# q and k of blocks 9 to 11 turned by transposing transfers on SyncE's queue

## The chip, the cores and the metric

One core of a Trainium2 chip. The metric is the device time of one execution in microseconds. TensorE (PE) multiplies and, in this kernel, also transposes; VectorE (DVE) and ScalarE (ACT) work on its results; GpSimd (POOL) and SyncE (SP) mostly issue transfers, each into a queue of its own that is worked off in order.

## The reference

Two stages. The first is a retention layer with a decaying state per head; the second a channel mix on its result. Batch 4, 8 heads, 768 tokens, head size 64; model width 512, hidden width 1024.

```python
for t in range(S):
    state = gamma[None, :, None, None] * state + np.einsum('bhd,bhe->bhde', k[:, :, t], v[:, :, t])
    y[:, :, t] = scale * np.einsum('bhd,bhde->bhe', q[:, :, t], state)
...
xk = mu_k * x + (1.0 - mu_k) * x_prev
xr = mu_r * x + (1.0 - mu_r) * x_prev
k = np.maximum(xk @ w_k, 0.0)
v = k * k @ w_v
r = 1.0 / (1.0 + np.exp(-(xr @ w_r)))
return (r * v)
```

## The kernel before, in words

The 4 x 768 tokens are cut into 12 blocks of 256 (three blocks to a batch, so 9, 10 and 11 are the last batch). The recurrence is done blockwise: inside a block as masked scores (k times q, masked, times v), from block to block through a carried state of 64x64 per head. Decay factors are put on v (`vs`), on the state (`G`, with the constants `gd`) and on the result (`gy`).

For a block, in short: `lq`, `lk`, `lv` load (the first two cast to fp16 on the way); `Tq`, `Tk` turn q and k on TensorE so that the head dimension lies on the partitions; `Eq`, `Ek` copy them from PSUM to the tiles `qT` and `kT` on ScalarE (L240); `S` are the scores (L317 for blocks 6 to 11), `M` the mask (L346); `C` is the block's own state (L365); `U` adds it to the carried one (L418), `G` decays that; `I` multiplies the carried state by q (L440), `Y` adds the scores times v (L461) and the other half of `I`; `D` scales into `xT`. Then the channel mix: `dx`, `X` (L557) mix tokens; `K` (L571, L581), `Qa` (L590), `Qb` (L598, L602) are the first product, the relu and the square; `R` (L611) and `s` (L617) the gate; `V` (L623) the second product, `O` (L629) the result, `st` (L636) the store.

Blocks 6 to 11 (`HALF`) do the first stage in 64x64 pieces, four of which use the four quarters of TensorE's array. Heads go in four pairs `j`; the partition half `a` of a head in a pair is given by `HEADS`. In odd pairs the two heads are swapped, so that in `I` the input half and the output half differ:

```python
HEADS = ((0, 1), (3, 2), (4, 5), (7, 6))
```

The whole program is one list, `ORDER`, written out by hand. A word is an operation, its block and further arguments; `~v`, `~a`, `~p`, `~s` name the engine (VectorE, ScalarE, GpSimd, SyncE), `@67` the PSUM banks. Words of one engine run in the order of the list, and each waits for its inputs and for the buffers that it overwrites. `qT` and `kT` have three buffers each, so block 10 takes the place of block 7, block 9 that of 6, block 11 that of 8. The results `os` have four. SyncE's queue carries the stores and, in the middle, `lv.11`; GpSimd's carries nearly all loads.

Of the kernel before, what the change touches and what calls it, by code (L numbers as in the profile page):

```python
# [10 lines left out]
F32 = mybir.dt.float32  # L11
# [11 lines left out]
HEADS = ((0, 1), (3, 2), (4, 5), (7, 6))  # L23
ORDER = """
cm gy.0~v mu~a lv.0~p lq.0.0.2~s lk.0.0.2~s ck.0.0.2~a cq.0.0.2~a z.12@6 Tq.0.0.2@0 Tk.0.0.2@1 gy.1~v
z.1@2 mt@2 Ek.0.0.2~a Eq.0.0.2~a S.0.1.0.2@01 S.0.0.0.2@45 me~a lk.0.2.4~p Tk.0.2.4@2 Ek.0.2.4~a
lq.0.2.4~p vs.0~v C.0@67 U.0.0~v Tq.0.2.4@3 Eq.0.2.4~a lq.1~p lk.1~p M.0.1.0.2~v z.2@2 S.0.1.2.4@23
U.0.1~v lv.1~p lk.2~p I.0@01 S.0.0.2.4@67 M.0.0.2.4~v wk.0~p wk.1~p G.0~a z.2@6 Tq.1@6 Eq.1~a vs.1~p
lq.2~p Tk.1@7 Ek.1~a M.0.0.0.2~v M.0.1.2.4~v Y.0 D.0~v t.0.0.3~a t.0.0.2~a t.0.0.1~a lv.2~p z.2@4
S.1.1@23 M.1.1~v C.1@01 U.1.0~v z.2@4 I.1@23 S.1.0@67 X.0.0.1~v t.0.1.2~a X.0.0.2~v Tk.2@0 t.0.1.3~a  # L30
t.0.0.0~a M.1.0~v X.0.0.0~v z.2@4 Y.1 t.0.1.1~a X.0.0.3~v Ek.2~a K.0.0@0 K.0.1@6 lq.4~p U.1.1~v
G.1~a wr~p lk.4~p D.1~v dx.1~v X.1.0.2~v X.1.0.0~v K.0.2@1 Qa.0.0~a Qb.0.0~a Qa.0.2~a lq.3~p
X.1.0.1~v X.1.0.3~v X.1.1.0~v Qa.0.1~a K.0.3@0 Qa.0.3~a lk.3~p vs.2~v Tq.2@1 X.1.1.2~v K.1.3@6
K.1.0@0 C.2@7 U.2.0~v lv.3~p Eq.2~a S.2.1@23 M.2.1~v S.2.0@45 M.2.0~v Qb.0.3~a lv.4~p K.1.1@1
X.1.1.1~v Qa.1.0~a t.0.1.0~a K.1.2@7 I.2@23 Qb.0.1~a Qa.1.1~a wv.0~p Qb.0.2~a Tq.4@01 Eq.4~a Y.2
Qa.1.3~a Qb.1.1~a X.0.1.3~v X.1.1.3~v R.1.1@4 Tk.4@01 Ek.4~a J.2 R.1.0@6 Qa.1.2~a s.1.0~a X.0.1.2~v
X.0.1.1~v X.0.1.0~v R.0.1@5 s.0.1~a s.1.1~a R.0.0@7 s.0.0~a S.4.1@01 Qb.1.0~a D.2~v dx.2~v X.2.0.2~v
X.2.0.0~v S.4.0@23 Tq.3@4 Eq.3~a X.2.0.1~v wv.1~p X.2.0.3~v Tk.3@7 lq.5~p Ek.3~a K.2.2@5 Qa.2.2~a
K.2.3@4 M.4.1~v M.4.0~v Qa.2.3~a Qb.2.3~a lk.6~p S.3.1@67 M.3.1~v S.3.0@01 vs.3~p C.3@23 U.3.0~a
Qb.2.2~a K.2.1@4 Qa.2.1~a K.2.0@2 Qa.2.0~a I.3@45 lq.6~p vs.4~v C.4@67 U.3.1~v X.2.1.1~v V.0.1.0@3  # L40
M.3.0~v V.1.0.0@2 G.3~a U.4.0~v I.4@01 X.2.1.3~v U.4.1~v J.3 Qb.1.3~a Y.4 Qb.2.0~a lk.5~p X.2.1.2~v
X.2.1.0~v Y.3 D.3~v dx.3~v V.0.0.0@7 V.0.1.1 O.0.1~v Tq.5@45 J.4 D.4~v dx.4~v R.2.0@6 Qb.2.1~a
V.0.0.1 O.0.0~v X.3.0.1~v Eq.5~a Qb.1.2~a V.1.0.1 X.3.0.2~v O.1.0~v Tq.6@01 Eq.6~a Tk.6@45 Ek.6~a
st.0.0~s lk.7~p st.1.0~s V.1.1.0@3 V.1.1.1 O.1.1~v s.2.0~a R.2.1@0 s.2.1~a lv.5~p X.3.0.0~v
X.3.0.3~v Tk.7@67 Ek.7~a G.4~a S.6@45 M.6~v Tk.5@23 Ek.5~a vs.5~v V.2.0.0@0 K.3.2@1 Qa.3.2~a K.3.0@6
S.5.0@23 M.5.0~v S.5.1@45 C.5@1 U.5.0~v K.3.3@7 Qb.3.2~a Qa.3.0~a lq.7~p K.3.7@6 Qa.3.3~a Qa.3.7~a
lv.6~p lq.8~p vs.6~v M.5.1~v V.2.0.1 st.0.1~s I.5@67 O.2.0~v st.2.0~s C.6@23 U.6.0~a U.6.1~v U.6.2~v
K.3.6@1 Qa.3.6~a lk.9~p X.3.1.3~v Y.5 Tq.7@45 Eq.7~a U.6.3~v X.3.1.2~v I.6@01 J.5 X.3.1.0~v D.5~v
X.3.1.1~v Qb.3.3~a G.6~a V.2.1.0@2 K.3.1@3 V.2.1.1 O.2.1~v Qb.3.7~a Qa.3.1~a Qb.3.1~a dx.5~v K.3.4@4
K.3.5@5 Qa.3.5~a X.5.0.0~v X.5.0.3~v R.3.1@2 s.3.1~a lv.7~p Qa.3.4~a X.5.0.1~v Qb.3.4~a R.3.0@5  # L50
R.4.0@2 s.3.0~a s.4.0~a Qb.3.0~a X.5.0.2~v vs.7~v K.5.2@4 S.7@67 st.1.1~s M.7~v Qb.3.5~a Y.6
Qb.3.6~a lv.10~p C.7@23 U.7.0~v X.5.1.1~v Qa.5.2~a K.5.0@5 R.4.1@6 Qa.5.0~a D.6~v s.4.1~a V.4.0.0@4
V.4.0.1 V.3.1.0@5 U.7.1~v Qb.5.0~a X.5.1.3~v U.7.2~v I.7@01 X.5.1.2~v U.7.3~v Tq.8@67 Eq.8~a
X.5.1.0~v O.4.0~v lv.8~p vs.8~v Qb.5.2~a lq.10~p lk.8~p Tk.8@23 Ek.8~a V.3.1.1 V.3.0.0@4 C.8@67
O.3.1~v st.2.1~s st.3.1~s Y.7 dx.6~v D.7~v Tq.10@23 V.3.0.1 Eq.10~a G.7~a dx.7~v X.6.0.2~v V.4.1.0@5
V.4.1.1 X.6.0.0~v R.5.0@0 R.5.1@1 K.5.3@2 Qa.5.3~a Qb.5.3~a O.3.0~v s.5.0~a K.5.1@4 X.6.0.1~v lq.9~p
lk.10~p Qa.5.1~a Qb.5.1~a lv.11~s s.5.1~a X.6.0.3~v K.6.3@2 Qa.6.3~a K.6.2@3 K.6.5@4 Qa.6.2~a
U.8.0~v Qa.6.5~a X.6.1.2~v V.5.0.0@0 st.3.0~s X.6.1.0~v K.6.4@1 Qa.6.4~a O.4.1~v U.8.1~v X.6.1.1~v
U.8.2~v I.8@45 S.8@67 Tk.10@23 Ek.10~a V.5.0.1 lv.9~p X.6.1.3~v vs.9~v K.6.6@1 Qb.6.2~a M.8~v
Qa.6.6~a Qb.6.5~a S.10@67 O.5.0~v Y.8 M.10~v D.8~v vs.10~v dx.8~v st.5.0~s st.4.0~s Tk.9@23 Ek.9~a  # L60
V.5.1.0@1 V.5.1.1 X.8.1.3~v vs.11~v O.5.1~v lk.11~p Qb.6.3~a Tk.11@23 Qb.6.4~a X.8.0.1~v X.8.0.3~v
lq.11~p Tq.11@67 Ek.11~a X.8.1.2~v Tq.9@45 Eq.9~a K.6.1@0 Qa.6.1~a Eq.11~a R.6.0@2 s.6.0~a K.6.7@4
R.6.1@5 s.6.1~a Qa.6.7~a C.9@23 S.11@67 X.8.0.0~v C.10@01 K.6.0@5 U.9.0~a Qa.6.0~a Qb.6.0~a U.9.1~v
X.8.0.2~v Qb.6.6~a U.9.2~v U.9.3~v G.9~v Qb.6.1~a R.7.0@4 s.7.0~a K.8.1@5 Qa.8.1~a K.8.0@3 Qa.8.0~a
R.7.1@2 s.7.1~a K.8.2@4 Qa.8.2~a V.6.0.0@3 U.10.0~v X.8.1.1~v U.10.1~v U.10.2~v st.4.1~s U.10.3~v
M.11~v G.10~v I.9@45 Qb.6.7~a C.11@67 S.9@01 M.9~v Qb.8.0~a V.6.0.1 V.7.1.0@2 V.7.1.1 U.11.0~v
U.11.1~v I.10@01 U.11.2~v I.11@67 O.6.0~v Y.9 D.9~v dx.9~v V.6.1.0@3 V.6.1.1 O.6.1~v K.8.3@4
Qa.8.3~a Qb.8.2~a Y.10 D.10~v dx.10~v X.9.0.3~v X.9.0.1~v X.9.0.0~v Y.11 X.9.0.2~v D.11~v st.5.1~s
st.6.1~s V.7.0.0@3 Qb.8.1~a V.8.0.0@4 V.8.1.0@5 Qb.8.3~a V.8.0.1 V.7.0.1 O.7.0~v O.7.1~v X.8.1.0~v
dx.11~v X.11.0.2~v V.8.1.1 K.9.4@0 K.9.6@1 K.9.5@6 Qa.9.5~a Qb.9.5~a K.9.1@3 K.9.7@2 Qa.9.7~a  # L70
Qb.9.7~a X.11.0.3~v X.11.1.0~v X.11.0.0~v R.8.0@6 K.9.0@2 s.8.0~a Qa.9.6~a Qa.9.0~a Qb.9.0~a K.9.2@7
K.9.3@1 Qa.9.2~a X.11.1.3~v X.11.0.1~v X.9.1.0~v K.11.0@2 Qa.11.0~a Qb.11.0~a R.8.1@7 Qb.9.2~a
s.8.1~a st.7.0~s st.6.0~s Qb.9.6~a O.8.0~v X.9.1.1~v K.11.3@2 K.11.1@4 X.9.1.2~v Qa.11.3~a X.9.1.3~v
R.10.1@7 K.11.2@6 R.9.1@2 Qa.9.3~a Qa.11.1~a O.8.1~v R.9.0@1 Qa.9.1~a Qb.9.1~a Qb.9.3~a V.9.1.0@3
Qb.11.1~a X.11.1.1~v X.11.1.2~v Qa.11.2~a V.10.0.0@4 V.10.1.0@6 Qa.9.4~a Qb.9.4~a V.10.1.1 R.11.0@0
s.9.0~a V.9.1.1 st.7.1~s V.9.0.0@1 V.9.0.1 st.8.1~s Qb.11.2~a V.10.0.1 s.9.1~a V.11.0.0@2 s.10.1~a
O.10.1~v O.9.1~v st.9.1~s R.10.0@3 O.9.0~v Qb.11.3~a st.9.0~s R.11.1@1 s.11.0~a V.11.0.1 st.10.1~s
Vc.11.1.1@0 O.11.0~v s.10.0~a st.8.0~s O.10.0~v s.11.1~a Oc.11.1.1~v Vc.11.1.0@1 st.10.0~s st.11.0~s
Oc.11.1.0~v sc.11.1.0~s sc.11.1.1~a
# [4 lines left out]
def kernel(  # L84
# [35 lines left out]
    gd_np = gam[np.array(HEADS).T[par // D]] ** TM  # L120
# [34 lines left out]
    csm = const.tile([P, 4 * H + (2 + LOG) * NJ + 2 * NCO + 3], F32, name="csm_sb")  # L155
# [15 lines left out]
    gd = csm[:, o : o + NJ]  # L171
    g0 = csm[:, o + NJ : o + 2 * NJ]
    pw = csm[:, o + 2 * NJ : o + (2 + LOG) * NJ].rearrange("p (l j) -> p l j", l=LOG)
    ident8 = csm[0 : 2 * NCO, o + (2 + LOG) * NJ : o + (2 + LOG) * NJ + 2 * NCO]
    mark = csm[:, o + (2 + LOG) * NJ + 2 * NCO :]
# [20 lines left out]
    def heads(j):  # L196
        return [(a, h, h // 2, h % 2) for a, h in enumerate(HEADS[j])]

# [21 lines left out]

    def load(x, d, split, a=None):
        def go(e, n, j0=0, j1=NJ):
            b, t0 = n // NB, n % NB * TM
            hs = slice(2 * j0, 2 * j1)
            src = x[b, hs, t0 : t0 + TM, :]
            dst = staged(a)[:, hs] if (a, n, j0) in EARLY else d(n)[:, hs]
            if split and (half(n) or wide(n)):
                for i in range(2):
                    e.dma_start(  # L229
                        out=dst[:, :, i * D : i * D + D],  # L230
                        in_=src[:, i * P : i * P + P].rearrange("h p d -> p h d"),
                    )
            else:
                e.dma_start(out=dst, in_=src.rearrange("h (p i) d -> p h (i d)", i=2))

        return go
# [26 lines left out]
    def trans(a):  # L263
        def go(e, n, j0=0, j1=NJ):
            pt = turned(n, a, j0)
            src = (K16 if a else Q16)(n)
            for j in range(j0, j1):
                for i in range(2):
                    if whole(n):
                        for s, h, jo, hp in heads(j):  # L270
                            nc.tensor.transpose(  # L271
                                pt[low(s), j, i, :], src[:, h, i * D : i * D + D], ident
                            )
                        continue
                    for u in range(2):
                        for s, h, jo, hp in heads(j):
# [19 lines left out]
    def turned_k(e, n, j0=0, j1=NJ):  # L296
# [6 lines left out]
        )  # L303

# [53 lines left out]
    def state_half(n):  # L358
        ps = banks("C", n).rearrange("p u (i j d) -> p u i j d", i=2, j=NJ)
        for j in range(NJ):  # L360
            for i in range(2):
                for u in range(2):
                    if more(n) or not (u and i):
                        for a, h, jo, hp in heads(j):
                            nc.tensor.matmul(  # L365
                                ps[low(a), u, i, j, :],
                                lhsT=K16(n)[low(u), h, i * D : i * D + D],
# [430 lines left out]
```

## Time and profile before

| | |
|---|---|
| runs | 153.82, 154.86, 154.31 us; median 154.31 |
| profiled execution | 154.38 us, of which the span is 152.6 us |
| TensorE busy | 144.1 us, 94% |
| VectorE busy | 128.7 us, 84% |
| ScalarE busy | 100.6 us, 66% |
| GpSimd busy | 55.3 us, 36% |
| chain that ended last | TensorE 91%, VectorE 3%, ScalarE 2% |
| DMA busy | 9 tenths or more up to about 84 us, little after |

The span is the time in the profiler's window; the execution's time has some 1.8 us around it. In the timelines, "PE" rows are matmuls, "PEld" weight loads, "SPq" rows the issuing of transfers by SyncE. A group's row gives its busy time, the mean length of one in ns, and after the bar the idle time ahead of it with what ended it.

### The profile page before, as it was taken

The page shows a single profiled execution, that of the slowest core. Times are in us where ns is not written, and L with a number is a line of the kernel's source. Part 1 is how long each engine was busy: PE and PEld are TensorE (multiplying, and loading weights), DVE is VectorE, ACT ScalarE, POOL GpSimd, SP SyncE. Part 2 cuts the span into 40 slices and gives each one's busy share as a digit, 9 for nine tenths or more (in the row PEclk, how much of TensorE's full clock was granted, in tenths as well). Part 3 has the DMA queues.
Part 4 walks back from the last instruction along what each step waited for, and adds up shares of the span by engine and source line. Part 5 has one row for each costly group of instructions (what it writes and reads, how often), then busy time and mean ns, then how long its engine had stood idle before and what let it go on. Part 6 is the DMA issues. An engine that isn't in the chain of part 4 may idle for free.

```text
span 152.6 us, 5532 instructions
## 1 busy us (share of the span) xinstructions
PE 144.1 (94%) x2426; PEld 82.9 (54%) x2426; DVE 128.7 (84%) x214; ACT 100.6 (66%) x187; POOL 55.3 (36%) x65
## 2 busy tenths in 40 slices
PE   7977799999999999999999999899999999999990
PEld 3354487758655554547554655557555445744450
DVE  7876999999999999999999999999789999702240
ACT  3466979899934894979483889879405048997130
POOL 7954988579867109997600000000000000000000
PEclk9999999999999999999999999999999999999999
DMA  5999999999999999999999203220002050010435
GB/s 137 215 224 200 207 229 194 170 249 210 196 167 207 236 250 112 290 275 203 206 191 225 83 0 136 81 73 0 4 4 75 0 205 1 14 54 4 158 117 206
DMA packets 45624, 22.16 MB, mean 145 GB/s; under 512 B 37400, under 2 KB 41248, under 8 KB 45600
## 3 DMA queue, kind: packets, MB, share of 16 engines
q0 software_dynamic: 38704, 14.42, 74.0%
q1 hardware_dynamic: 6592, 7.21, 13.7%
q8 instruction: 19, 0.31, 0.8%
q10 hardware_dynamic: 304, 0.18, 0.5%
q14 instruction: 5, 0.04, 0.1%
HBM read 24.16 MB, written 6.29 MB: 200 GB/s over the span
## 4 chain that ended last, share of the span: by engine, by line
PE 91%; DVE 3%; ACT 2%; issue 1%; DVEq 0%
PE ps L623 27%; PE ps L581 14%; PE ps L611 14%; PE ps L571 14%; PE ps L701 4%; PE ps L277 3%; PE ps L440 2%; PE ps L271 2%; DVE a L353 2%; PE ps L330 1%; PE ps L477 1%; ACT qT L240 1%; PE ps L317 1%; PE ps L461 1%; PE ps L641 1%; PE ps L365 1%
## 5 line engine op out<-in xcount | busy, mean ns | idle before, releaser
L623 PE MATMUL ps<-wv,k2s 128*128 128x512 f16 x184 | 43.3, 380 | 0.0
L590 ACT ACTIVATE kr<-ps 128x512 f32<-128x512 f32 x48 | 27.4, 596 | 21.5 <-PE ps L581 11.1
L623 PEld LDWEIGHTS <-k2s 128*128 128x128 f16 x184 | 17.0, 98 | 19.3 <-ACT k2s L602 0.2
L629 DVE SCALAR_TENSOR_TENSOR os<-ps,rs 128x512 f32<-128x512 f32 x23 | 15.5, 685 | 12.4 <-ACT rs L617 7.1
L611 PE MATMUL ps<-wr,xr 128*128 128x512 f16 x96 | 23.5, 379 | 0.0
L581 PE MATMUL ps<-xk,wk 128*128 128x256 f16 x192 | 23.4, 273 | 0.0
L571 PE MATMUL ps<-xk,wk 128*128 128x512 f16 x96 | 22.9, 379 | 0.0
L229 POOL DMA_DIRECT2D k<-in_k_dram x20 | 17.9, 908 | 11.1 <-PE ps L383 6.8
L581 PEld LDWEIGHTS <-wk 128*128 128x128 f16 x192 | 18.3, 98 | 4.4 <-issue 0.2
L240 ACT COPY qT<-ps 128x1024 f16<-128x1024 f16 (+1 forms) x13 | 12.4, 951 | 9.2 <-PE ps L277 7.8
L557 DVE SCALAR_TENSOR_TENSOR xr<-dx,mu,xT 128x256 f16<-128x256 f32 (+1 forms) x32 | 18.0, 579 | 0.1
L617 ACT ACTIVATE rs<-ps 128x512 f32<-128x512 f32 x24 | 13.7, 594 | 6.1 <-DVE os L629 3.2
L229 POOL DMA_DIRECT2D v<-in_v_dram x18 | 16.0, 904 | 3.6 <-DMA wr<-in_moe_w_r_dram 1.9
L557 DVE SCALAR_TENSOR_TENSOR xk<-dx,mu,xT 128x256 f16<-128x256 f32 (+1 forms) x32 | 17.1, 581 | 0.2
L353 DVE TENSOR_TENSOR a<-ps,c_sb 128x1024 f16<-128x1024 f32 (+1 forms) x14 | 14.6, 1066 | 0.7 <-PE ps L338 0.4
L602 ACT ACTIVATE k2s<-kr 128x512 f16<-128x512 f32 x24 | 14.6, 626 | 0.2
L571 PEld LDWEIGHTS <-wk 128*128 128x128 f16 x96 | 9.1, 98 | 10.3
L611 PEld LDWEIGHTS <-xr 128*128 128x128 f16 x96 | 9.1, 98 | 10.2 <-DVE xr L557 0.3
L598 ACT ACTIVATE k2s<-kr 128x512 f16<-128x512 f32 x24 | 14.4, 625 | 0.3
L240 ACT COPY kT<-ps 128x1024 f16<-128x1024 f16 (+1 forms) x13 | 12.3, 944 | 2.9 <-PE ps L271 2.0
L528 DVE TENSOR_TENSOR dx<-xT 128x1024 f32<-128x1024 f32 x11 | 13.5, 1223 | 0.3
L252 DVE TENSOR_TENSOR vs<-v,csm_sb 128x1024 f16<-128x1024 f32 x10 | 12.2, 1219 | 0.2 <-DMA v<-in_v_dram 0.2
(74 smaller groups left out, 165.5 us busy)
## 6 DMA issues: line engine op xcount, KB each, us to landing
out_dram<-os SPq DMA_DIRECT2D x23, 256.0 KB, 3.0
v<-in_v_dram POOLq DMA_DIRECT2D x18, 256.0 KB, 7.3
q<-in_q_dram POOLq DMA_DIRECT2D x11, 256.0 KB, 7.8
k<-in_k_dram POOLq DMA_DIRECT2D x21, 128.0 KB, 8.9
v<-in_v_dram POOLq DMA_DIRECT2D x2, 512.0 KB, 7.1
wk<-in_moe_w_k_dram POOLq DMA_DIRECT2D x2, 512.0 KB, 11.2
wv<-in_moe_w_v_dram POOLq DMA_DIRECT2D x2, 512.0 KB, 9.7
wr<-in_moe_w_r_dram POOLq DMA_DIRECT2D x1, 512.0 KB, 9.3
```

What stands on the lines that cost most here:

```text
L229: e.dma_start(out=dst[:, :, i * D : i * D + D], in_=src[:, i * P : i * P + P].rearrange("h p d -> p h d"),)
L240: e.copy(out=out, in_=in_)
L353: nc.vector.tensor_tensor(out=a_full(n)[:, i, :, j0:j1], in0=pairs(banks("S", n, i, j0))[:, :, j0:j1], in1=(below if wide(n) else causal[: ...
L557: nc.vector.scalar_tensor_tensor(out=XM[w](k)[:, j, t0:t1], in0=DX(k)[:, j, t0:t1], scalar=mu[:, w * NCO + j : w * NCO + j + 1], in1=x[:, ...
L571: nc.tensor.matmul(banks("K", n, g), lhsT=wk16[:, co, g * P : g * P + P], rhs=XM[0](k)[:, co, :], start=(co == 0), stop=(co == NCO - 1),)
L581: nc.tensor.matmul(pz[:, i, :], lhsT=wk16[:, co, fo * P : fo * P + P], rhs=XM[0](k)[:, co, m * TM + t0 : m * TM + t1], start=(i == 0 and c ...
L590: nc.scalar.activation(out=kr, in_=banks("K", n, g, *u), func=AF.Relu)
L598: nc.scalar.activation(out=k2s[:, n % 3 : n % 3 + 2, g, :], in_=kr, func=AF.Square,)
L602: nc.scalar.activation(out=K2(n)[:, w * g : w * g + w, t0:t1], in_=kr.rearrange("p a t -> p (a t)").rearrange("p (i t) -> p i t", i=w), fu ...
L611: nc.tensor.matmul(banks("R", n, tb), lhsT=XM[1](k)[:, co, t : t + P], rhs=wr16[:, co, :], start=(co == 0), stop=(co == NCO - 1),)
L623: nc.tensor.matmul(banks("V", n, tb), lhsT=K2(n)[:, fo, tb * P : tb * P + P], rhs=wv16[:, fo, :], start=(fo == 0), stop=(fo == NFO - 1),)
L629: nc.vector.scalar_tensor_tensor(out=OS(2 * n + tb), in0=banks("V", n, tb), scalar=1.0 / (KSC * KSC), in1=RS(2 * n + tb), op0=ALU.mult, op ...
```

## The change

For blocks 9, 10 and 11 (`TURNED`), q and k are no longer transposed on TensorE and copied out by ScalarE. Instead `Dq` and `Dk` issue, on SyncE's queue, eight transposing transfers each, from the loaded tile straight into `qT` or `kT`: 48 transfers of 128x128 fp16. For that, q and k of these blocks are loaded with the two halves of a block apart (`by_half`; `C` reads k from there too), so q comes in two transfers where it came in one. Heads of these blocks are not swapped in odd pairs (`heads(n, j)`), with decay constants to match, and the first write into a PSUM bank in `intra_half` starts it where `I` did not. The constant masks `cm` are named in three words instead of one, on the same engine and in the same order.

```diff
+TURNED = (9, 10, 11)
 ORDER = """
-cm gy.0~v mu~a
+cm.0~v cm.1~v cm.2~v gy.0~v mu~a
...
-O.3.1~v st.2.1~s st.3.1~s Y.7 dx.6~v D.7~v Tq.10@23 V.3.0.1 Eq.10~a G.7~a
+O.3.1~v st.2.1~s st.3.1~s Y.7 dx.6~v D.7~v V.3.0.1 Dq.10~s G.7~a
...
-U.8.2~v I.8@45 S.8@67 Tk.10@23 Ek.10~a V.5.0.1
+U.8.2~v I.8@45 S.8@67 Dk.10~s V.5.0.1
...
-st.5.0~s st.4.0~s Tk.9@23 Ek.9~a V.5.1.0@1
+st.5.0~s st.4.0~s Dk.9~s V.5.1.0@1
...
-lk.11~p Qb.6.3~a Tk.11@23 Qb.6.4~a X.8.0.1~v X.8.0.3~v
-lq.11~p Tq.11@67 Ek.11~a X.8.1.2~v Tq.9@45 Eq.9~a K.6.1@0 Qa.6.1~a Eq.11~a R.6.0@2
+lk.11~p Qb.6.3~a Qb.6.4~a X.8.0.1~v X.8.0.3~v
+lq.11~p Dk.11~s X.8.1.2~v Dq.9~s K.6.1@0 Qa.6.1~a Dq.11~s R.6.0@2
...
-    def heads(j):
-        return [(a, h, h // 2, h % 2) for a, h in enumerate(HEADS[j])]
+    def heads(n, j):
+        order = (2 * j, 2 * j + 1) if n in TURNED else HEADS[j]
+        return [(a, h, h // 2, h % 2) for a, h in enumerate(order)]
...
+    def by_half(x):
+        return x.rearrange("p h x -> p (h x)").rearrange("p (i h d) -> p i h d", i=2, h=H)
...
+            if n in TURNED and a is not None:
+                dst = by_half(d(n))
+                for i in range(2):
+                    e.dma_start(out=dst[:, i], in_=src[:, i * P : i * P + P].rearrange("h p d -> p h d"))
+                return
...
+    def turned_by_dma(a):
+        def go(e, n):
+            src, dst = by_half((K16 if a else Q16)(n)), (KT if a else QT)(n)
+            for j in range(NJ):
+                for i in range(2):
+                    e.dma_start(
+                        out=dst[:, j, i, :], in_=src[:, i, 2 * j : 2 * j + 2].rearrange("p h d -> p (h d)"),
+                        transpose=True,
+                    )
+
+        return go
...
     def intra_half(n):
         py = pairs(banks("I", n))
+        fresh = {0, 1} if n in TURNED else set()
...
-                            start=False, stop=False, skip_group_check=True,
+                            start=(u == hp and hp in fresh), stop=False, skip_group_check=True,
                         )
+                        if u == hp:
+                            fresh.discard(hp)
```

More of the change, by code (lines that the diff above doesn't have):

```diff
@@ L23 @@
 HEADS = ((0, 1), (3, 2), (4, 5), (7, 6))
+TURNED = (9, 10, 11)
 ORDER = """
[L25 to L75, printed above, removed]
@@ L119 @@
     h_pj = 2 * np.arange(NJ)[None, :] + (par // D)[:, None]
-    gd_np = gam[np.array(HEADS).T[par // D]] ** TM
+    gd_np = np.stack([gam[np.array(HEADS).T[par // D]], gam[h_pj]], axis=1) ** TM
     g0_np = 0.125 * KSC / KUP * gam[h_pj] ** (1 - TM)
@@ L154 @@
     c16 = const.tile([P, 4 * P + W], F16, name="c16_sb")
-    csm = const.tile([P, 4 * H + (2 + LOG) * NJ + 2 * NCO + 3], F32, name="csm_sb")
+    csm = const.tile([P, 4 * H + (3 + LOG) * NJ + 2 * NCO + 3], F32, name="csm_sb")
     gy = const.tile([P, NJ, TM], F32, name="gy_sb")
@@ L170 @@
     gks = csm[:, 0:o].rearrange("p (w i h) -> p w i h", w=2, i=2)
[L171 to L175, printed above, removed]
+    gd = csm[:, o : o + 2 * NJ].rearrange("p (w j) -> p w j", w=2)
+    o += 2 * NJ
+    g0 = csm[:, o : o + NJ]
+    o += NJ
+    pw = csm[:, o : o + LOG * NJ].rearrange("p (l j) -> p l j", l=LOG)
+    o += LOG * NJ
+    ident8 = csm[0 : 2 * NCO, o : o + 2 * NCO]
+    mark = csm[:, o + 2 * NCO :]
     count = OS(3)[:, 0:P]
@@ L269, in go @@
                     if whole(n):
-                        for s, h, jo, hp in heads(j):
+                        for s, h, jo, hp in heads(n, j):
                             nc.tensor.transpose(
@@ L275, in go @@
                     for u in range(2):
-                        for s, h, jo, hp in heads(j):
+                        for s, h, jo, hp in heads(n, j):
                             nc.tensor.transpose(
@@ L363, in state_half @@
                     if more(n) or not (u and i):
-                        for a, h, jo, hp in heads(j):
+                        for a, h, jo, hp in heads(n, j):
                             nc.tensor.matmul(
                                 ps[low(a), u, i, j, :],
-                                lhsT=K16(n)[low(u), h, i * D : i * D + D],
+                                lhsT=by_half(K16(n))[low(u), i, h] if n in TURNED
+                                else K16(n)[low(u), h, i * D : i * D + D],
                                 rhs=VS(n)[low(u), i, h],
@@ L380, in state @@
                 for i in range(2 if more(n) else 1):
-                    for a, h, jo, hp in heads(j):
+                    for a, h, jo, hp in heads(n, j):
                         o = ps[low(a)]
@@ L391, in state @@
                 for u in range(2 if more(n) else 1):
-                    for a, h, jo, hp in heads(j):
+                    for a, h, jo, hp in heads(n, j):
                         o = ps[low(a)]
@@ L420, in decayed @@
     def decayed(e, n):
+        g = gd[:, int(n in TURNED)]
         if e is nc.scalar:
@@ L423, in decayed @@
                 nc.scalar.activation(
-                    out=TG[0](n + 1)[:, j], in_=T32(n)[:, j], func=AF.Copy, scale=gd[:, j : j + 1]
+                    out=TG[0](n + 1)[:, j], in_=T32(n)[:, j], func=AF.Copy, scale=g[:, j : j + 1]
                 )
@@ L427, in decayed @@
         e.tensor_tensor(
-            out=TG[0](n + 1), in0=T32(n), in1=gd[:, :, None].to_broadcast([P, NJ, D]), op=ALU.mult
+            out=TG[0](n + 1), in0=T32(n), in1=g[:, :, None].to_broadcast([P, NJ, D]), op=ALU.mult
         )
@@ L436, in inter @@
             for i in range(parts):
-                for a, h, jo, hp in heads(j):
+                for a, h, jo, hp in heads(n, j):
                     u = a ^ s
@@ L459, in intra_half @@
                 for u in range(2):
-                    for a, h, jo, hp in heads(j):
+                    for a, h, jo, hp in heads(n, j):
                         nc.tensor.matmul(
@@ L475, in intra @@
                 for i in range(2):
-                    for a, h, jo, hp in heads(j):
+                    for a, h, jo, hp in heads(n, j):
                         nc.tensor.matmul(
@@ L486, in intra @@
                 for u in range(2):
-                    for a, h, jo, hp in heads(j):
+                    for a, h, jo, hp in heads(n, j):
                         nc.tensor.matmul(
@@ L671, in constants, with masks @@
             nc.vector.tensor_scalar_add(out=count[:, m : 2 * m], in0=count[:, 0:m], scalar1=float(m))
-    def masks(e):
+    def masks(e, part):
         for out, col, op in (
-            (ident, 0, ALU.is_equal), (causal[:, 0], 1, ALU.is_ge), (causal[:, 1], 1, ALU.is_gt),
-            (step, 2, ALU.is_ge), (below, 0, ALU.is_ge),
-        ):
-            nc.vector.tensor_scalar(
+            ((ident, 0, ALU.is_equal),),
+            ((causal[:, 0], 1, ALU.is_ge), (causal[:, 1], 1, ALU.is_gt)),
+            ((step, 2, ALU.is_ge), (below, 0, ALU.is_ge)),
+        )[part]:
+            e.tensor_scalar(
                 out=out, in0=count[:, 0 : out.shape[-1]], scalar1=mark[:, col : col + 1], scalar2=None, op0=op
@@ L744 @@
         "cq": cast(0), "ck": cast(1),
-        "Tq": trans(0), "Tk": trans(1), "Eq": turned_q, "Ek": turned_k,
+        "Tq": trans(0), "Tk": trans(1), "Dq": turned_by_dma(0), "Dk": turned_by_dma(1), "Eq": turned_q, "Ek": turned_k,
         "S": scores, "M": masked, "C": state, "U": summed, "G": decayed, "I": inter_off, "Y": intra, "J": inter_on,
```

5 lines of the change are left out of this document (1 added, 4 removed).

## The prediction

> **What bounds the kernel now.** I read the page first: shares of busy time and the chain of work that ended last.
>
> ```profile
> span 152.6 us, 5532 instructions
> PE 144.1 (94%) x2426; PEld 82.9 (54%) x2426; DVE 128.7 (84%) x214; ACT 100.6 (66%) x187; POOL 55.3 (36%) x65
> PE 91%; DVE 3%; ACT 2%; issue 1%; DVEq 0%
> ```
>
> TensorE is the bound: it is busy for 94% of the span and holds 91% of the chain. A microsecond of TensorE work taken out of a gapless stretch is a microsecond gained, as long as nothing else arrives late; any wait put in front of TensorE, which takes its instructions in order, is a microsecond lost. So I went to the chain in order of time, where this change acts (columns: start, length, what).
>
> ```profile
> 79.02 0.28 PE ps L277 x30
> ...
> 90.33 0.27 PE ps L277 x32
> ...
> 93.21 0.03 PE ps L277
> ...
> 93.24 0.28 PE ps L277 x30
> ...
> 95.35 0.31 PE ps L277 x24
> 95.67 0.45 issue
> 96.11 0.80 PE ps L277 x72
> ...
> 100.47 0.38 PE ps L365 x32
> 100.84 0.29 PE ps L317 x32
> ```
>
> L277 is the transposing matmul. These rows are `Tq.10`, `Tk.10`, `Tk.9` (two rows), and `Tk.11`, `Tq.11`, `Tq.9` in one run with an issue gap inside. L317 at 100.84 is `S.11`, the scores of block 11, the first work that needs block 11 turned. After it the span has 152.6 - 100.84 = 51.8 us left.
>
> **What is removed.** The rows above are all 192 transposes of blocks 9 to 11: 0.28 + 0.27 + 0.03 + 0.28 + 0.31 + 0.45 + 0.80 = 2.42 us of TensorE's chain. All lie before `S.11`, so TensorE would now want to start `S.11` at 100.84 - 2.42 = 98.42. The evictions `Eq` and `Ek` leave ScalarE (the group of those to kT between 74 and 102 us; 1010 ns is the mean of one):
>
> ```profile
> L240 ACT COPY kT<-ps 128x1024 f16<-128x1024 f16 x4 | 4.0, 1010 | 0.9 <-PE ps L277 0.9
> ```
>
> Six of them at about 1.01 us are 6 us, but ScalarE holds 2% of the chain, so I give nothing for them beyond what TensorE saves.
>
> **What is added.** Each `Dq` or `Dk` is eight transfers of 128x128 fp16 (32 KB); six of them are 48, all issued by SyncE's queue in its order. That queue also carries the stores and one load. Its order is now: `st.3.1`, `Dq.10`, `lv.11` (two loads), `st.3.0`, `Dk.10`, `st.5.0`, `st.4.0`, `Dk.9`, `Dk.11`, `Dq.9`, `Dq.11`, `st.4.1`. The timeline of that queue in the run before (start, length, what):
>
> ```profile
> 78.39 0.33 SPq L636 DMA_DIRECT2D out_dram<-os  x1
> ...
> 78.83 0.39 SPq L229 DMA_DIRECT2D v<-in_v_dram  x1
> ...
> 79.31 0.63 SPq L229 DMA_DIRECT2D v<-in_v_dram  x1
> ...
> 84.43 0.36 SPq L636 DMA_DIRECT2D out_dram<-os  x1
> ...
> 92.86 0.36 SPq L636 DMA_DIRECT2D out_dram<-os  x1
> ...
> 93.27 1.79 SPq L636 DMA_DIRECT2D out_dram<-os  x2
> ...
> 93.75 1.31 SPq L636 DMA_DIRECT2D out_dram<-os  x1
> ```
>
> The first row is `st.3.1`, then the two parts of `lv.11`, `st.3.0`, `st.5.0` (92.86), `st.4.0` (93.27) and, next in the queue, `st.4.1` (93.75). What holds the queue until 92.86 is the result that `st.5.0` stores (VectorE's timeline):
>
> ```profile
> 92.15 0.69 DVE L629 SCALAR_TENSOR_TENSOR os<-ps,rs 128x512 f32<-128x512 f32 x1
> ```
>
> The removed transposes do not bring that forward much: VectorE is full there (4.86 of 5.00 us, in the stretches shown with the loads). So `Dk.9`, `Dk.11`, `Dq.9` and `Dq.11`, 32 transfers, stand in line from **93.75** on. `S.11` needs the last of them. Only 98.42 - 93.75 = 4.67 us lie between.
>
> **The price of one transfer.** No transposing transfer stands in the trace, so I bound it. The stores, taken as a group (min/median/max of an issue in ns; then us from issue to landing), give the issue time of large plain transfers and the landing:
>
> ```profile
> L636 SPq DMA_DIRECT2D out_dram<-os x23: 332/357/1311, 50.1 to 148.6; - x23
> ...
> DMA to landing us min/median/max: 2.0/3.0/6.4
> ```
>
> The lower bound is the shortest issue, 0.33 us; the upper one the longest, 1.31 us. A gain below 0.33 is not excluded by any row and is carried as a rival. I take **0.63 us**, the row of the second `lv.11` load: it is the nearest, a transfer of many short pieces issued directly behind another of its kind, as 31 of the 32 will be. For the last landing I take the median, 3.0 us (bounds 2.0 and 6.4).
>
> [...]
>
> Step by step: the last issue ends at 93.75 + 32 x 0.63 = 113.91; it lands at 116.91; `S.11` starts there instead of at 100.84, 16.07 us later. Everything that TensorE has queued behind `S.11` (`C.10`, `K.6.0`, the gates of 7, `K.8`, all later values) waits with it, and VectorE, ScalarE and the stores wait for TensorE; the remaining 51.8 us follow unchanged, since they were a gapless TensorE chain already.
>
> Ahead of that, `Dq.10` starts when block 7's last use of that buffer is done (TensorE's timeline),
>
> ```profile
> 78.69 0.33 PE L440 MATMUL ps<-qT,tg 64*64 64x64 f16 x16
> ```
>
> at 79.02, so eight end at 84.06, `lv.11` at 85.1, `st.3.0` at 85.4, `Dk.10` at 90.5, landed at 93.5. `S.10` stood at 92.4 and would now want 0.55 us earlier, so it waits about 1.6 us; the stall at `S.11` swallows that, and `st.5.0` does not hang on it.
>
> **The halves no longer swapped.** Only L440 (the carried state times q) is touched: in odd pairs its output half differed from its input half, so successive pairs used other quarters of the array; now all use the same two. In the chain:
>
> ```profile
> 75.62 0.26 PE ps L440 x16
> ...
> 89.81 0.26 PE ps L440 x16
> 90.06 0.27 PE ps L317 x31
> ```
>
> Sixteen of L440 take as long as 31 of L317, which use all four quarters, so they run nearly two wide already. Blocks 9 to 11 have 24 + 32 + 32 = 88 of them, 1.43 us; the cost lies between 0 and a doubling, 1.43. I take 0.5, since the quarters alternated only from one pair of heads to the next.
>
> **The loads.** q of the three blocks now comes in two transfers each, with rows of half the length.
>
> ```profile
> 74.79 0.88 POOL L234 DMA_DIRECT2D q<-in_q_dram  x1
> ```
>
> is the last issue of GpSimd's timeline. The queue of the loads between 60 and 100 us (packets, MB, share of 16 engines), and then 5 us stretches of the core (per engine its busy time; the last two columns are the DMA share and GB/s):
>
> ```profile
> q0 software_dynamic: 10997, 3.80, 75.0%
> ```
>
> ```profile
> 80.00:85.00 5.00, 5.00 (x32) 2.83 (x30) 4.83 (x8) 1.73 (x6) 0.00 (x0) 1.00 0.93 188
> 85.00:90.00 5.00, 5.00 (x57) 2.42 (x57) 5.00 (x11) 4.50 (x10) 0.00 (x0) 1.00 0.14 52
> 90.00:95.00 5.00, 5.00 (x200) 2.93 (x186) 4.86 (x6) 4.52 (x7) 0.00 (x0) 1.00 0.26 96
> ```
>
> There are three more issues of 0.88 us on GpSimd, which has nothing after 75.67, and up to 1024 more packets each. In the stretch from 60 to 100 us the load queue used 75% of 16 engines for 10997 packets, 43.6 ns each, so 3072 more would be 8.4 us of DMA time if packets set the price, and nothing if bytes do. The DMA share falls from 0.93 to 0.14 at about 85, so the loads would end by 93 at the worst, before `Dk.11` is due to be issued (98.8). I cost it at nothing; if the load of k 8, queued right behind q 10, were pushed past its use, TensorE would lose at most the 0.88 + 2.8 us of that one load, inside the range. The three parts of `cm` stay on VectorE in the same order: nothing.
>
> **Sum**, against the profiled execution (154.38 us, span 152.6, so 1.78 around it): 154.38 + 16.07 + 0.5 = 170.95; it lies 0.07 over the median of the runs shown: **171.0 us**. Low: 0.33 and 2.0 give 93.75 + 10.56 + 2.0 = 106.31, or +5.5: 159.8. High: with 1.31 the queue reaches `Dk.9` at 79.02 + 10.48 + 1.02 + 0.36 + 10.48 + 0.84 = 102.2, and 32 x 1.31 + 6.4 end at 150.5, +49.7 and 1.4: 205.5.
>
> **Rivals.** *One after the other.* If each transposing transfer starts only when the one before has landed, a piece costs the landing, at least 2.0 us. For it: many small transfers into one tile; against it: the queue before had `st.4.0` issued 0.41 us after `st.5.0`, far under a landing. Then `Dq.10` ends at 95.0, `Dk.10` at 112.4, and 64 us more from 113.2 end at 177.2: +76.4, **231 us**.
>
> *Hidden after all (the other side).* If the queue takes the pieces at almost no cost, the transposes vanish behind other work. It decides at (4.67 - 2.0) / 32 = 0.083 us a piece. Then the gain is the 2.42 less 0.5: **152.5 us**. For it: the transfer engines are nearly idle (0.14 and 0.26 above). Against it: no issue of this queue took under 0.33. [...]
>
> *No change.* Between 0.09 and 0.2 us a piece, or with pieces hidden but VectorE, 4.86 of 5.00 us busy there, giving nothing back, the time stays at about **154.3 us**.
>
> **How the numbers follow.** Queue-bound as forecast: 0.80. One after the other: 0.12. Hidden: 0.05. No change: 0.03. The range 159 to 205 holds the first case and leaves out the others, 0.20. A change of 1% is about what a measurement of this kernel can tell from none. Faster 0.05, same 0.03, slower 0.92.
>
> **What would show it.** The changed profile should show 48 transfers on SyncE's queue at about 0.63 us each, back to back from 93.75 to 114; a hole of about 17 us in TensorE ahead of `S.11`, released by a transfer into qT; a smaller one of 1 to 2 us ahead of `S.10`; no L240 on ScalarE for blocks 9 to 11; and after `S.11` the same 52 us. I am wrong if the pieces are far from 0.63, if the hole stands elsewhere (at `Tk.8`: the loads), or if TensorE runs slower after the hole.

## The result, and the profile after

The changed kernel takes 204.27 us (median of 4 runs, 202.09 to 204.40) against 154.17 for the kernel before (153.82 to 154.86): a ratio of 1.321, interval 1.311 to 1.331. The profiled execution took 204.2 us, its span 202.4. The sign and the place were as forecast; the loss is 50 us where 16.6 were forecast. In the experiments below a median is over all runs, and a ratio leaves out the runs over 1.5% above the fastest of the same kernel, so the two can differ a little.

The page of the kernel after: span, TensorE's share, its busy tenths, the clock granted to it and the DMA share in 40 slices, and the chain by engine.

```profile
span 202.4 us, 5225 instructions
PE 149.1 (74%) x2234; PEld 84.5 (42%) x2234; DVE 129.2 (64%) x214; ACT 95.4 (47%) x181; POOL 57.9 (29%) x68
PE   7877999699999999995249200001279999999992
PEclk9999999999999999999658855555559999999999
DMA  6999999999969999916131111111130010401054
...
PE 43%; SPq 26%; DMA 11%; POOL 8%; DVE 6%; issue 4%; DVEq 0%; POOLq 0%
```

TensorE held 91% of the chain; now it holds 43%, and SyncE's queue 26%. Two holes are open in TensorE's row. In the longer one, from 113 to 148 us, the transfer engines are busy for 0.13 of the time (the stretch is shown below), while the queue issues without a break until 147.1. That queue's timeline:

```profile
80.50 10.39 SPq L269 DMA_TRANSPOSE qT<-q  x8
90.99 1.65 SPq L188 DMA_DIRECT2D v<-in_v_dram  x2
92.73 0.86 SPq L612 DMA_DIRECT2D out_dram<-os  x1
93.70 10.02 SPq L269 DMA_TRANSPOSE kT<-k  x8
103.82 1.00 SPq L612 DMA_DIRECT2D out_dram<-os  x2
104.86 21.56 SPq L269 DMA_TRANSPOSE kT<-k  x16
126.55 20.51 SPq L269 DMA_TRANSPOSE qT<-q  x16
147.11 51.74 SPq L612 DMA_DIRECT2D out_dram<-os  x13
```

From 80.5 to 147.1 the queue does nothing but issue, back to back. Sixteen transfers in 20.51 us are 1.28 us each, not 0.63. One of them, taken as a group (min/median/max of an issue in ns; us to landing):

```profile
L269 SPq DMA_TRANSPOSE qT<-q x24: 1099/1182/1417, 80.5 to 145.9; - x24
...
DMA to landing us min/median/max: 2.3/2.3/4.5
```

1.18 us are the instruction itself, 0.1 the step to the next. The landing, 2.3 us counted from the start of the issue, is longer than the step, so two are under way at a time. And what waited for them (total, times, longest):

```profile
PE ps L288 <- DMA qT<-q: 33.8, 8, 26.7
...
PE ps L288 <- DMA kT<-k: 9.4, 8, 3.1
```

L288 are the scores. The 9.4 us are `S.10`, one wait for each piece of `Dk.10`; the 33.8 are `S.11`. The end of that wait, in the chain in order of time:

```profile
145.88 2.33 DMA qT<-q
148.25 0.27 PE ps L288 x4
148.52 0.43 PE ps L336 x19
148.94 1.82 PE ps L547 x4
150.77 1.71 PE ps L587 x4
```

The last four matmuls of `S.11` come at 148.25, where `S.11` stood at 100.84: 47.41 us of the 49.8 by which the span grew. The rest follows at once. Four matmuls of L547 take 1.82 us and four of L587 1.71, where these groups took 0.97 and 0.86 before: TensorE's granted clock is still 0.50 after the hole, from 148 to 152 us.

```profile
113.00:148.00 35.00, 1.88 (x28) 1.06 (x29) 2.83 (x8) 0.58 (x2) 0.00 (x0) 0.53 0.13 26
```

This stretch of the core (busy time of the five engines, then granted clock, DMA share, GB/s) shows TensorE busy for 1.88 of 35 us and its granted clock at 0.53; whether the clock is the cause is tested last. The two groups cost 0.85 us each over before.

### The profile page after: what moved, and what is told of

It is laid out like the page before. It is cut to its first block, busy times and chain, and to the rows that moved or that the text cites. A ratio compares the mean times of both kernels' runs of the same rounds, so it can differ in the third digit from the quotient of the medians.

```text
span 202.4 us, 5225 instructions
## 1 busy us (share of the span) xinstructions
PE 149.1 (74%) x2234; PEld 84.5 (42%) x2234; DVE 129.2 (64%) x214; ACT 95.4 (47%) x181; POOL 57.9 (29%) x68
## 4 chain that ended last, share of the span: by engine, by line
PE 43%; SPq 26%; DMA 11%; POOL 8%; DVE 6%; issue 4%; DVEq 0%; POOLq 0%
SPq L269 24%; PE ps L599 15%; DMA v<-in_v_dram 10%; PE ps L547 9%; PE ps L587 7%; PE ps L557 5%; POOL q L193 2%; POOL k L188 2%; POOL vs L211 2%; PE ps L413 1%; DVE xT L482 1%; DVE dx L504 1%; DMA qT<-q 1%; PE ps L236 1%; SPq L612 1%
## 5 line engine op out<-in xcount | busy, mean ns | idle before, releaser
L599 PE MATMUL ps<-wv,k2s 128*128 128x512 f16 x184 | 44.4, 387 | 0.0
L288 PE MATMUL ps<-qT,kT 64*64 64x64 f16 x192 | 6.0, 212 | 43.2 <-DMA qT<-q 33.8
L390 DVE TENSOR_TENSOR tg<-ps,tg 128x256 f16<-128x256 f32 x20 | 8.4, 420 | 34.5 <-PE ps L336 33.1
L587 PE MATMUL ps<-wr,xr 128*128 128x512 f16 x96 | 24.4, 390 | 0.0
L547 PE MATMUL ps<-xk,wk 128*128 128x512 f16 x96 | 23.7, 390 | 0.0
L288 PEld LDWEIGHTS <-kT 64*64 64x64 f16 x192 | 3.7, 112 | 45.7 <-issue 28.7
L317 DVE TENSOR_TENSOR a<-ps,c_sb 128x1024 f16<-128x1024 f32 x6 | 7.3, 1222 | 13.3 <-PE ps L288 13.3
L587 PEld LDWEIGHTS <-xr 128*128 128x128 f16 x96 | 9.4, 100 | 10.8 <-issue 1.4
L547 PEld LDWEIGHTS <-wk 128*128 128x128 f16 x96 | 9.3, 99 | 10.9 <-issue 0.5
```

The source lines that it names most:

```text
L547: nc.tensor.matmul(banks("K", n, g), lhsT=wk16[:, co, g * P : g * P + P], rhs=XM[0](k)[:, co, :], start=(co == 0), stop=(co == NCO - 1),)
L587: nc.tensor.matmul(banks("R", n, tb), lhsT=XM[1](k)[:, co, t : t + P], rhs=wr16[:, co, :], start=(co == 0), stop=(co == NCO - 1),)
L599: nc.tensor.matmul(banks("V", n, tb), lhsT=K2(n)[:, fo, tb * P : tb * P + P], rhs=wv16[:, fo, :], start=(fo == 0), stop=(fo == NFO - 1),)
```

## The experiments

**What sets the price of a piece: the amount, or the instruction?** In `e1_twelve` the 48 transfers are joined to twelve.

```diff
-            for j in range(NJ):
-                for i in range(2):
-                    e.dma_start(
-                        out=dst[:, j, i, :], in_=src[:, i, 2 * j : 2 * j + 2].rearrange("p h d -> p (h d)"),
-                        transpose=True,
-                    )
+            for i in range(2):
+                e.dma_start(
+                    out=dst[:, :, i, :], in_=src[:, i].rearrange("p h d -> p (h d)"), transpose=True,
+                )
```

> The 48 transfers are joined to 12: one for each half of a block (128 tokens by all 8 heads, 128 KB), same places in the queue. Theory A, each transposing transfer costs SyncE about 1.28 us whatever it holds: the twelve take 15 us in all, the eight of Dk.9 to Dq.11 end near 105.5 and land near 108, S.11 waits some 9 us, and the time is about 162 us. Theory B, the price goes by the amount that is turned (1.28 us for 32 KB): each of the twelve takes about 5.1 us, the queue is as long as with 48, and the time stays at about 204 us.

Measured: 163.8 us, ratio 1.059 (1.054 to 1.064). In its queue:

```profile
93.76 6.76 SPq L268 DMA_TRANSPOSE kT<-k  x4
100.62 5.13 SPq L268 DMA_TRANSPOSE qT<-q  x4
```

and as a group:

```profile
L268 SPq DMA_TRANSPOSE qT<-q x6: 1205/1214/2079, 79.1 to 104.5; - x6
```

Four times the data in a transfer, 1.21 us against 1.18. Theory A holds: **the price is the instruction's**, and theory B falls. Of the 1.8 us above theory A's 162, 1.6 are again TensorE's two first groups behind the hole. The 6.76 us hold one issue of 2.79, the first behind two stores. Such issues stand in the traces of the changed kernel (2.30 us), `e1_twelve` (2.79 and 2.08), `e4_k_only` (1.91 and 1.92) and `e5_six` (2.59), mostly the first or second behind stores; in `e6_six_early` the longest is 1.38. Why is not shown.

**Is it the price of a small transfer, or of transposing?** `e2_plain` takes the transposition out and leaves everything else.

```diff
-                        transpose=True,
```

> The same 48 transfers without the transposition: plain copies of the same 128x128 pieces (q and k of blocks 9 to 11 are then not turned, so the scores of these blocks are of other numbers). If the price is that of a small transfer on this queue, they take 1.2 to 1.3 us each and the time stays near 204 us. If it is that of transposing, they take 0.33 to 0.45 us each as the stores and loads do, S.11 waits some 10 to 12 us and the time is 163 to 167 us.

Measured: 172.51 us in its one run. The queue of that kernel, and one transfer as a group:

```profile
104.74 10.43 SPq L269 DMA_DIRECT2D qT<-q  x16
```

```profile
L269 SPq DMA_DIRECT2D qT<-q x24: 470/551/1480, 79.3 to 114.6; - x24
```

A step of 0.65 us. The expected 0.33 to 0.45 was too low: one such copy takes 0.55 us to issue, a store 0.36 before; why is not shown. But 0.65 is close to what the prediction had taken from the `lv.11` row for a *transposing* transfer. So 0.63 fits a small plain transfer (by luck, since that row is a load of 256 KB), and the step of a transposing one, 1.28, is twice that.

**Is it all the queue?** `e3_tensor_unswapped` turns blocks 9 to 11 on TensorE again and leaves the rest of the change in:

```diff
-... Dq.10~s ... Dk.10~s ... Dk.9~s ... Dk.11~s ... Dq.9~s ... Dq.11~s
+... Tq.10@23 ... Eq.10~a ... Tk.10@23 Ek.10~a ... Tk.9@23 Ek.9~a ... Tk.11@23 ... Tq.11@67 Ek.11~a ... Tq.9@45 Eq.9~a ... Eq.11~a
```

> The transposing transfers alone are undone: blocks 9 to 11 are turned by TensorE and copied out by ScalarE again, in the places of before, while the heads stay unswapped and q comes in two loads of halves. The prediction's terms for these two were 0.5 us (0 to 1.43) and nothing (up to 3.7): 154.2 to 155.6 us, 154.7 expected. If the unswapped halves or the longer loads carried a part of the 50 us, it would be well above 157 us.

Measured: 155.26 us against 154.52, ratio 1.002 (0.997 to 1.007). The unswapped halves and the longer loads are not where 50 us went. `e4_k_only` halves the dose: q back on TensorE, k by transfers.

```diff
-... Dq.10~s ... Dq.9~s ... Dq.11~s
+... Tq.10@23 ... Eq.10~a ... Tq.11@67 ... Tq.9@45 Eq.9~a ... Eq.11~a
```

> Half the dose: k of blocks 9 to 11 turned by transfers (24), q by TensorE and ScalarE as before. If the delay is the queue's, 24 pieces at 1.28 us: Dk.10 lands near 98.5, Dk.9 and Dk.11 start near 97 and land near 120, S.11 starts some 19 us later than in the kernel before, and with 2.4 us of slow clock behind the hole the time is about 175 us. If the delay came from something that the first of these transfers switches on, it would stay close to 204 us.

Measured: 175.67 us, one run.

```profile
84.96 10.75 SPq L276 DMA_TRANSPOSE kT<-k  x8
...
96.90 21.65 SPq L276 DMA_TRANSPOSE kT<-k  x16
```

The queue starts the sixteen at 96.90 and ends them at 118.55 (expected: 97, and landed near 120): the delay follows the count of pieces.

**Can the transposes be hidden when they are few?** `e5_six` makes one transfer of a whole block: `qT` and `kT` of these blocks hold the halves outside the pairs, and the scores and the carried state read them so.

```diff
+            e.dma_start(
+                out=dst.rearrange("c j i t -> c (j i) t"), in_=src.rearrange("p i h d -> p (i h d)"),
+                transpose=True,
+            )
...
+    def by_ij(n, x):
+        if n not in TURNED:
+            return x
+        return x.rearrange("c j i t -> c (j i t)").rearrange("c (i j t) -> c j i t", i=2, j=NJ)
```

> One transposing transfer for a whole block of q or k (256 tokens by 8 heads, 256 KB), six in all, same places in the queue. If an issue costs 1.28 us whatever it holds, the last four run from 93.8 to 99, land at about 101.5, and S.11 starts 0.7 us later than in the kernel before: about 155.2 us. If the price begins to go by the amount (a transfer of eight times the first size), each takes visibly over 1.3 us and the time is above 157 us.

Measured: 159.57 us, one run; a miss by 4.4.

```profile
93.73 4.01 SPq L272 DMA_TRANSPOSE kT<-k  x2
97.85 2.68 SPq L272 DMA_TRANSPOSE qT<-q  x2
```

```profile
L272 SPq DMA_TRANSPOSE qT<-q x3: 1237/1271/1365, 79.1 to 99.3; - x3
...
DMA to landing us min/median/max: 3.1/3.2/3.3
```

The issue is 1.27 us even for 256 KB, eight times the first size, so its price hardly goes by the amount. But `Dk.9`, right behind the two stores, took 2.59 us (in the 4.01 above), and the landing grew from 2.3 to 3.2, so `S.11` began at 102.4. The hole of 3.6 us ahead of it again brought the half clock (0.50 from 103 to 107 us), which was not in the expectation.

`e6_six_early` also moves the two stores behind the six transfers.

```diff
-... dx.8~v st.5.0~s st.4.0~s Dk.9~s ... Dq.11~s R.6.0@2
+... dx.8~v Dk.9~s ... Dq.11~s st.5.0~s st.4.0~s R.6.0@2
```

> The six, with the two stores st.5.0 and st.4.0 moved behind them in SyncE's queue, so that nothing holds the last four: they should have landed by 97, before TensorE wants S.11 (98.4). Theory P: TensorE is the only bound, so the whole 2.4 us of transposes is gained: 152.0 us. Theory V: VectorE, full from 80 to 103 us, is the next bound (K.8 needs X.8.0.2, which ended at 102.70 in the kernel before while K.8 began at 103.26), so no more than about 0.6 us is gained: 153.7 to 154.3 us.

Measured: 154.75 us against 154.35, ratio 1.003 (0.9995 to 1.006). The transposes are hidden now: TensorE's timeline has `S.11` right behind `C.9`, without a wait for a transfer:

```profile
98.52 0.45 PE L339 MATMUL ps<-vs,k 64*64 64x64 f16 x32
98.79 0.46 PE L291 MATMUL ps<-qT,kT 64*64 64x64 f16 x32
```

But nothing is gained, and the chain in order of time says where it went:

```profile
94.07 0.69 DVE xT L485
...
95.46 1.22 DVE vs L216
96.67 1.15 DVE dx L507
...
98.25 0.83 DVE vs L216
...
99.39 0.69 DVE os L608
...
100.12 0.44 PE ps L339 x30
```

VectorE carries the chain from 94 to 100 us; TensorE stands 0.82 us at `C.10` for a bank that VectorE's `O.5.1` frees. Theory P falls; theory V is borne out, though the time lies a little above its 153.7 to 154.3. Two runs tried to use that. `e7_six_early_pool` moves the scaling of v (`vs`) of these blocks to GpSimd, and `e8_before_pool` does only that to the kernel before.

```diff
-... vs.9~v ... vs.10~v ... vs.11~v ... lq.11~p
+... lq.11~p vs.9~p vs.10~p vs.11~p
```

> As e6_six_early, and the scaling of v of blocks 9 to 11 (three times 1.22 us) goes from VectorE to GpSimd, which has nothing after its last load. Under theory V this frees VectorE by 3.7 us where it is full and the gain of the transposes comes through: 152.0 to 152.7 us. Under theory P it changes nothing against e6_six_early. If GpSimd's work slows VectorE, it stays at 153.5 or above.

> The control for it: the kernel before, with only the scaling of v of blocks 9 to 11 moved from VectorE to GpSimd. TensorE's chain is gapless there with the transposes in it, so both theories say no change, 154.0 to 154.7 us; if it gained 1 us or more, the gain of e7_six_early_pool would not be the transposes'.

Measured: 156.84 us, ratio 1.010 (1.005 to 1.016), and for the control 155.85, ratio 1.008 (1.005 to 1.010). Two runs of `e7_six_early_pool` took 154.84 and 155.41 us at a granted clock of 1.00, four took 156.83 to 157.42 at 0.989. The profiled one, of 157.42 us, had 0.73 from 85 to 90 us, where TensorE was busy for 3.02 of the 5. The control lost too: its timeline of VectorE, while GpSimd ran two `vs` from 79.94 to 84.68,

```profile
79.61 1.49 DVE L506 TENSOR_TENSOR xT<-ps,gy_sb 128x512 f32<-128x512 f32 x2
81.13 1.79 DVE L528 TENSOR_TENSOR dx<-xT 128x1024 f32<-128x1024 f32 x1
82.96 2.93 DVE L557 SCALAR_TENSOR_TENSOR xk<-dx,mu,xT 128x512 f16<-128x512 f32 x2
```

against the same three before:

```profile
79.60 1.49 DVE L506 TENSOR_TENSOR xT<-ps,gy_sb 128x512 f32<-128x512 f32 x2
81.12 1.23 DVE L528 TENSOR_TENSOR dx<-xT 128x1024 f32<-128x1024 f32 x1
82.38 1.42 DVE L557 SCALAR_TENSOR_TENSOR xk<-dx,mu,xT 128x512 f16<-128x512 f32 x2
```

Beside GpSimd's work VectorE was slower: the two groups with two inputs in SBUF took 1.79 us instead of 1.23 and 2.93 instead of 1.42, the one that reads PSUM 1.49 as before. It cost just the engine that was to be relieved, and TensorE with it, which in the control waited 1.91 us for VectorE at `K.6` and in the kernel before not at all:

```profile
85.00:90.00 5.00, 3.46 (x20) 1.95 (x20) 5.00 (x10) 3.85 (x8) 0.00 (x0) 1.00 0.14 52
```

TensorE is busy for 3.46 of the 5 us there, where it was busy for all 5 before.

`e9_six_early_order` keeps all on VectorE and only reorders it; `e10_before_order` is its control.

```diff
-V.5.1.1 X.8.1.3~v vs.11~v O.5.1~v ... X.8.0.2~v
+V.5.1.1 O.5.1~v X.8.1.3~v ... X.8.0.2~v vs.11~v
```

> As e6_six_early, with VectorE's list put in the order in which TensorE needs it: the result O.5.1 ahead of X.8.1.3, and the scaling vs.11 behind X.8.0.2 instead of ahead of O.5.1. In e6_six_early TensorE stood 0.82 us at C.10 for that O.5.1. Theory V (VectorE holds back what the transposes give): that wait goes and the span falls by 0.5 to 1.0 us, 153.3 to 153.9 us. The rest of the 2.4 us should stay lost to the unswapped halves (some 0.8 us over L440's three blocks) and to VectorE. Without theory V: no change against e6_six_early, 154.3 to 154.8.

> The control: the kernel before with only that order of VectorE's list. TensorE has no gap there, so no change is expected: 153.9 to 154.6 us. A gain of 0.7 us or more would mean that e9_six_early_order owes its gain to the order alone.

Measured: 154.41 us against 154.32, ratio 1.0004 (0.998 to 1.002); the control 155.09, ratio 1.005 (1.003 to 1.008). The wait at `C.10` is gone, and another stands in its place a step on:

```profile
PE ps L560 <- DVE t L393: 0.8, 1, 0.8
```

`K.8` now waits for VectorE. Parity is the best that these runs reached; none beat the kernel before. That the order alone cost 0.5% was not expected; in the control, too, TensorE waits 0.5 us at `K.8` for VectorE, and in the kernel before it does not. So the new order only moved the wait. Against that control, `e9_six_early_order` is 0.7 us faster.

Another part of the 2.42 us goes to the unswapped halves. L440's 88 matmuls of blocks 9 to 11, by windows of that line alone, before and then in `e9_six_early_order` (L416 there; the first two numbers are the window, then TensorE's busy time):

```profile
100.84:152.60 51.76, 1.75 (x88) 1.24 (x88) 1.00 0.19 68
```

```profile
98.00:152.40 54.40, 2.41 (x88) 1.92 (x88) 0.99 0.19 69
```

2.41 - 1.75 = 0.66 us. In the chains, `e9_six_early_order` is 0.97 us ahead of the kernel before behind the first `K.8` products (104.08 against 105.05), and 0.33 at the end of the last matmuls (148.22 against 148.55), which fits. The 1.45 us lost ahead of that are the 0.8 at `K.8` and smaller losses that were not traced one by one.

**Is the slow stretch behind the hole the clock?** `e11_twelve_warm` is `e1_twelve` with matmuls on zeros in the hole (`z.24@6`, six of them), `e12_twelve_warmer` with eight.

```diff
-C.9@23 S.11@67
+C.9@23 z.24@6 S.11@67   (z.32@6 in e12_twelve_warmer)
```

> As e1_twelve, with six matmuls on zeros into a PSUM bank that S.11 starts anew, put between C.9 and S.11, where TensorE stood idle for 7.4 us (98.8 to 105.8). They fill some 5.5 us of it and hold nothing up. If the slow stretch behind the hole (S.11 to the end took 55.2 us against 51.8 before) is TensorE's clock falling while it idles, it shrinks to 51.8 to 52.6 us and the time falls from 163.8 to 160.5 to 161.5 us. If it is work that piled up, nothing changes.

Measured: 163.64 us, one run: a miss. Stretches of 2 us show why (columns as above, the clock third from the end):

```profile
104.00:106.00 2.00, 0.50 (x5) 0.21 (x5) 0.00 (x0) 0.00 (x0) 0.00 (x0) 1.00 0.51 103
106.00:108.00 2.00, 1.09 (x63) 0.81 (x63) 0.37 (x2) 0.00 (x0) 0.00 (x0) 1.00 0.77 264
108.00:110.00 2.00, 2.00 (x7) 0.76 (x6) 1.93 (x6) 1.18 (x3) 0.00 (x0) 0.57 0.11 35
```

The clock held at 1.00 while the zeros ran. It fell at about 108.3, after TensorE had next to nothing from 104.3 to 106.9.

> As e11_twelve_warm, with eight of the matmuls on zeros instead of six (7.2 us, to about 106.1), since there the granted clock still fell to 0.57 from 108 to 112, after TensorE had been nearly idle from 104.3 to 106.9. If the fall follows that idle time with a lag, the idle time left (0.8 us) is too short, the clock stays at 1.00, the first four-matmul groups behind S.11 take 0.86 to 0.97 us instead of 1.11 to 1.82, and the time is 161.5 to 162.3 us. If the clock falls whatever TensorE does there, it is 163.3 us or more again.

Measured: 160.96 us, one run.

```profile
108.00:110.00 2.00, 2.00 (x18) 1.65 (x17) 1.97 (x4) 1.97 (x5) 0.00 (x0) 1.00 0.00 0
```

and in its chain behind `S.11`:

```profile
106.55 0.97 PE ps L545 x4
107.52 0.86 PE ps L585 x4
```

The clock stays, and the first groups take 0.97 and 0.86 us as before the change. It is the clock. (The time lies 0.5 us under the expected range. Of the 2.7 us gained on `e11_twelve_warm`, 1.65 are the first three groups; another 1.0 came because `Dq.11` landed earlier.) For the fall in `e11_twelve_warm` a stretch of 2.6 us with four small matmuls in it was enough, and in `e5_six` the clock fell 2.1 us into the hole.

## Why the prediction was right and wrong

*What bounds the kernel, and where it would break*: right. TensorE in front of `S.11`, held by the last piece of `Dq.11`, at the end of SyncE's queue.

*The price of one transfer*: **this step failed.** I took 0.63 us from the `lv.11` row as the nearest; it is about the price of a plain copy of these pieces (`e2_plain`: 0.65). A transposing one costs 1.28 from one to the next, and hardly more when it holds more (1.31 in `e1_twelve`, 1.4 in `e5_six`). No row of the trace could show that; the upper bound of 1.31 held, and by it the time came out at 205.5. That this is so near to 204.27 is in part luck: it has 6.4 us behind the last issue, where 1.15 were left, and its line starts at 102.2 instead of 104.86.

*The start of the line at 93.75*: wrong as a consequence. At 0.63 the store `st.5.0` sets it; at 1.28 `Dk.10` only begins then, and `Dk.9` starts at 104.86. The first piece also came at 80.50 instead of 79.02: this execution was 1.5 us late from 36 us on, before the change does anything (a load of v landed later; in `e1_twelve`, with the same loads, the first piece came at 79.11).

*Landing*: 2.3 us instead of 3.0. The sum also added it behind the end of the last issue, while the profile counts it from the start (145.88 to 148.21): behind the end at 147.06 only 1.15 us were left. *The wait at `S.10`*: 9.4 us instead of 1.6, swallowed by `S.11` as said.

*"The remaining 51.8 us follow unchanged"*: wrong by 2.3. From the first matmuls behind `S.11` (148.94) to the end of the last ones (198.40) are 49.46 us, before (101.43 to 148.55) 47.12. Of the 2.34, 1.70 are the clock, which the sum had not got (the prediction named it among the signs of being wrong), and 0.66 the unswapped halves, put at 0.5.

*The loads at nothing*: held within the error of `e3_tensor_unswapped` (-0.3 to +0.7%, the unswapped halves included).

*The rivals*: one after the other fell, since the step (1.28 us) is shorter than the landing (2.3). Hidden after all fell for 48 pieces. With six early ones they are hidden, and the condition named under "no change" decides: VectorE, full at that place, gives nothing back.

## What to carry to other kernels

A new kind of instruction can have a price of its own (here 1.28 us, where the neighbour's row said 0.63): a neighbour's row in the trace is a bound, not a price, and the sum should be tried at both ends before a middle is chosen. Where the price is per instruction, count instructions: 48, 12 and 6 transfers moved the same bytes for 204, 164 and (issued early) 155 us. And before work is taken off the bounding engine, look at what the second engine does in that very stretch: VectorE, busy for 4.96 of the 5 us from 95, was the next bound, and 2.4 us saved on the first came out as nothing.

## What the runs showed of the hardware

A transposing transfer occupied the issuing queue for 1.18 us at 32 KB (the changed kernel), 1.21 at 128 KB (`e1_twelve`) and 1.27 at 256 KB (`e5_six`; medians of those of q); a plain one of 32 KB for 0.55 (`e2_plain`). It landed 2.3 us after the start of its issue at 32 KB (median) and 3.1 to 3.8 at 256 KB.

TensorE's granted clock, read from stretches of 0.5 us in the changed kernel and of 2 or 4 us in the others (an edge is laid where the mean of its stretch puts it), was at half from 97.8 to 108.0 and from 114.9 to 152.4 in the changed kernel, from 101.0 to 111.3 in `e1_twelve`, from 100.9 to 107.7 in `e5_six` and from 108.3 to 111.7 in `e11_twelve_warm`. These are 10.2, 37.5, 10.2, 6.8 and 3.4 us, close to 3, 11, 3, 2 and 1 times the last; no run shows why. The clock fell 2.1 to 4.1 us after TensorE ran out of work, and rose 3.1 to 5.3 us after the work resumed; a hole of 3.6 us (`e5_six`) brought 0.50, and so did one of 35. No long hole was needed: in `e11_twelve_warm` it fell behind two waits of 1.3 and 1.1 us with four small matmuls between them.

Beside GpSimd's elementwise work in `e8_before_pool`, VectorE's operations on two SBUF inputs took 1.79 us instead of 1.23 and 2.93 instead of 1.42.
